# A fused attention + two-layer FFN kernel: for units 8 to 23 the output, state, carried product and the next unit's scores become one piece, and score quarters above the diagonal are left out

## Chip, cores, metric

One core of a Trainium2 chip. The metric is device time in microseconds of one execution; three runs of the kernel before and one profiled execution are known.

## The reference

Gated linear attention with a per-channel decay, over 4 batches, 8 heads, 768 tokens and head width 48, then two feed-forward layers (384 to 2048 to 384) over the 3072 rows of 384:

```
for t in range(S):
    state = alpha[:, :, t, :, None] * state + np.einsum('bhd,bhe->bhde', k[:, :, t], v[:, :, t])
    y[:, :, t] = np.einsum('bhd,bhde->bhe', q[:, :, t], state)
...
h = x @ w_in ; g = np.maximum(0.01 * h, h) ; x = g @ w_out
h = x @ w_in ; g = np.where(h > 0.0, h, alpha * (np.exp(np.minimum(h, 0.0)) - 1.0)) ; g @ w_out
```

## The kernel before

**Units.** The 3072 tokens are cut into 24 units of 128. Six units make a batch; c is a unit's place in it, and at c = 0 no state comes in. The 8 heads go as 4 pairs, on partitions 0 to 47 and 64 to 111 (112 rows). For a unit u, VectorE (DVE) makes two scans over alpha: E from the right, whose product with the keys is kS, and F from the left, whose product with the queries is q. TensorE (PE) then makes

- the scores kS' q, in two PSUM tiles `sc0` and `sc1`. A pair's 128 keys x 128 queries of one head are two matmuls of 64 keys each (`attn_scT`), so the 48-row, 64-column matmuls of two heads and two key halves stand in four quadrants of the array: 16 matmuls a unit, 4 in each quadrant. All of the square is computed; the mask (DVE, `mask_half`, two instructions with the 0/1 tile `causal`) then clears the half above the diagonal and writes A.
- the carried product q times the state that comes in (`carried`), 8 matmuls, into the output tile `po`. It stands right behind the scores.
- `pk`, four transposes of kS; ScalarE (ACT) copies it out as `kn`.
- the output, `po` += A v (8 matmuls), and the new state's part `pu` = kn v (8 matmuls).

ACT then copies `po` out as the high part xh (three instructions), and DVE subtracts it from `po` for the low part xl (three, `attn_xl`); DVE adds the state S = pu + carried and makes the next `carried` = S pe. An fp32 matmul of these runs as two passes, which the trace counts as two instructions. Feed-forward matmuls are fp32r, 128x512, in high and low parts: three terms in place of one product.

**Order.** Four units make a block of 512 tokens, and feed-forward layer 1 runs over a block in 16 steps m. A step s issues nine hp matmuls for the step s + 2, the activation of that (ACT t, DVE max, ACT gh, DVE gl), then the attention's piece for this step, and then nine y matmuls of step s. Every engine keeps the order in which the program is written. Units 0 to 11 and layer 1 of blocks 0 and 1 stand in a list written out by hand (`STARTUP`, about 0 to 200 us); from then on the loop has three pieces for each unit in one step each (about 200 to 434 us, units 12 to 23):

```
def attn_pe(u, i):   # i: piece
    0: attn_scT(u)            (scores, carried product)
    1: attn_pk(u)
    2: attn_po(u), attn_pu(u)
def attn_post(u, i):
    0: masks of u, then E, pe, kS of u + 1
    1: kn of u, then F, q of u + 1
    2: xh, S, carried for u + 1, xl; at a block's end xl and the gather come first
```

Layer 2 (434 to 906 us) follows and is not touched. In the loop a step has one bank for hp; y has 3 banks, the pool `ps_a` ("at") has 3, and a further one, h1, takes half of `po`. In the loop sc0, sc1, `pk`, the other half of `po`, and `pu` take the three "at" banks in turn. gh has two buffers: gh of step s + 2 is written when y of step s has read its own.

**Transfers.** Unit u + 3's pack (alpha, k, q) and values vt are loaded behind piece 2 of u, one DMA each, by ACT's queue (by SP's at a block's end). At a block's end ten DMAs on SP gather the fourth group of rows into the other three (`gather`). At each batch's start a GpSimd (POOL) memset pads vt (L138); POOL also clips pe (L157).

Of the kernel before, what the change touches and what calls it, by code (L numbers as in the profile page):

```python
# [19 lines left out]
def attention_two_layers_kernel(  # L20
# [12 lines left out]
    nc = tc.nc  # L33
# [29 lines left out]
    causal = const.tile([128, C], F32, name="causal")  # L63
    minus = const.tile([PR, PR], F32R, name="minus")
# [8 lines left out]
    both = [[wts.tile([128, 2 * DM], F32R, name=f"w{i}_{m}") for i in range(2)] for m in range(KF)]  # L73
    win = [[t[:, 0:DM].rearrange("p (c f) -> p c f", f=128) for t in both[m]] for m in range(KF)]
# [10 lines left out]

    def constants():
        make_identity(nc, ident)
        nc.scalar.activation(minus, ident[0:PR, 0:PR], ACTF.Copy, scale=-1.0)
        nc.gpsimd.memset(causal, 1.0)
        nc.gpsimd.affine_select(  # L90
            out=causal, in_=causal, compare_op=ALU.is_ge, fill=0.0,
            base=0, pattern=[[1, C]], channel_multiplier=-1,
        )
# [20 lines left out]
    def load_unit(u, first=False, eng=None):  # L114
        t = pack_p.tile([PR, EXT + 2 * NP * C], F32, tag="pack", name="pack")
        if first:
            m = EXT + NP * C
            nc.sync.dma_start(t[:, 0:EXT], seqs[u, :, 0:EXT])
            nc.scalar.dma_start(t[:, EXT:m], seqs[u, :, EXT:m])
# [15 lines left out]
    def load_v(u, eng=None):  # L135
# [70 lines left out]
    def mask_half(u, j):  # L206
# [3 lines left out]
        nc.vector.tensor_mul(d["A"][:, j], d["sc"][j], causal.unsqueeze(1).to_broadcast([128, NP, C]))  # L210
# [18 lines left out]

    def attn_scT(u):  # L230
        d = st[u]
        kS, qh = d["kS"], d["qh"]
# [19 lines left out]

    def attn_po(u):
        c = u % NC
        d = st[u]
        vt = vts[u]
        A, qh = d["A"], d["qh"]
        if u < EARLY:
            d["po"] = [ps_a.tile([PR, NP, C], F32, tag="at", name="po")]
        t = d["po"]  # L260
        n = len(t)
        for p in range(NP):
            for j in range(2):
                o, dst = part(t, p, j)
                c0, wide = (3 * p + 2 * j) * D, D if o or (n == 2 and c > 0) else 64
                nc.tensor.matmul(dst[0:wide], lhsT=vt[:, c0:c0 + wide], rhs=A[:, j, p],  # L266
                                 start=(p < n and (n == 1 or c == 0)), stop=(p >= NP - n and (n == 2 or c == 0)),
                                 skip_group_check=True)
        if c > 0 and n == 1:
            for p in range(NP):  # L270
                for j in range(2):
                    r = slice(64 * j, 64 * j + D)
                    nc.tensor.matmul(t[0][r, p], lhsT=d["T"][r, p], rhs=qh[r, p],
                                     start=False, stop=(p == NP - 1), skip_group_check=True)

    def attn_pu(u):
# [138 lines left out]
    def ffn1_g(j, m):  # L415
# [6 lines left out]
        more.0 E.0 pe.0 F.0 kS.0 q.0 E.1 warm.3 sc.0 mask1.0 mask0.0 pe.1 kS.1 F.1 E.2 q.1 pe.2 kS.2 F.2 pk.0 warm.3  # L422
        po.0 kn.0 xh.0 pk.1 pu.0 warm.6 sc.1 rest.0 kn.1 S.0 xl.0 T.1 warm.2 pk.2 kn.2 mask0.1 mask1.1 pu.1 E.3 po.1
        q.2 pe.3 S.1 more.1 stage.1 F.3 kS.3 sc.2 more.3 more.2 T.2 xh.1 warm.3 rest.1 mask0.2 mask1.2 pk.3 pu.2 E.4
        q.3 pe.4 S.2 po.2 sc.3 p1.0 xl.1 F.4 kS.4 kn.3 mask1.3 mask0.3 T.3 xh.2 warm.4 rest.2 pu.3 pk.4 xl.2 kn.4
        p2.0 po.3 xh.3 E.5 q.4 sc.4 rest.3 pe.5 S.3 and.0 F.5 j1.0 kn.5 warm.2 pu.4 mask0.4 mask1.4 T.4 po.4 xl.3
        gather.0 stage.2 kS.5 j2.0 q.5 S.4 E.6 and.1 sc.5 hi.0 hA.0.0.7 p1.1 p2.1 T.5 xh.4 kS.6 mask1.5 mask0.5 pe.6
        pk.6 lo.0 F.6 j1.1 hB.0.0 rest.4 po.5 and.2 q.6 t.0.0 sc.6 max.0.0 p1.2 kn.6 xl.4 more.4 stage.3 j2.1 xh.5
        j1.2 gh.0.0 p2.2 hi.1 yA.0.0 rest.5 hA.0.1 pu.6 mask1.6 mask0.6 lo.1 E.7 hB.0.1 j2.2 kS.7 po.6 gl.0.0 pe.7
        pk.7 F.7 q.7 p2.3 S.6 hi.2 hA.0.2 yB.0.0 t.0.1 xl.5 xh.6 kn.7 T.7 p1.3 lo.2 and.3 sc.7 hB.0.2 rest.6 pu.7  # L430
        mask0.7 mask1.7 max.0.1 po.7 j1.3 j2.3 more.5 stage.4 xl.6 gh.0.1 t.0.2 yA.0.1 xh.7 hi.3 rest.7 hA.0.3
        gl.0.1 max.0.2 lo.3 xl.7 gh.0.2 gather.1 yB.0.1 yA.0.2 hB.0.3 stage.5 p2.4 p1.4 t.0.3 gl.0.2 and.4 j1.4 j2.4
        max.0.3 and.5 E.8 hA.1.0 hA.1.1 hB.1.0 stage.6 hB.1.1 yB.0.2 hA.1.2 hB.1.2 hi.4 t.1.0 t.1.1 p1.5 gh.0.3 p2.5
        t.1.2 max.1.0 pe.8 j1.5 gl.0.3 j2.5 max.1.1 lo.4 max.1.2 and.6 S.7 yA.0.3 yB.0.3 hA.1.3 p2.6 yc.0.3.0 gh.1.0
        yc.0.3.1 p1.6 yc.0.3.2 hi.5 gh.1.1 gl.1.0 j1.6 j2.6 F.8 lo.5 gl.1.1 stage.7 hA.1.4 hB.1.4 hB.1.3 yA.1.0
        and.7 t.1.3 hi.6 p1.7 gh.1.2 p2.7 t.1.4 yB.1.0 j1.7 hA.1.5 yA.1.1 hB.1.5 yB.1.1 lo.6 j2.7 gl.1.2 max.1.4
# [10 lines left out]
        hB.0.13 yA.0.9 hB.0.12 max.0.11 gl.0.9 and.15 yB.0.9 pu.8 j1.14 j2.14 gl.0.10 E.10 p2.15 t.0.13 yA.0.10
        gh.0.11 p1.15 t.0.12 kn.9 hi.14 j1.15 sc.8 yB.0.10 yA.0.11 hA.0.14 S.8 q.9 kS.10 max.0.12 lo.14 hB.0.14
        pe.10 gl.0.11 mask0.8 max.0.13 j2.15 mask1.8 carry.9 pu.9 po.8 gh.0.12 t.0.14 hi.15 gh.0.13 more.8 more.9
        gl.0.12 max.0.14 lo.15 hA.0.15 yB.0.11 hB.0.15 pk.10 yA.0.12 hA.1.8 yB.0.12 S.9 gl.0.13 sc.9 hB.1.8 yA.0.13  # L450
# [641 lines left out]
```

## Time and profile before

| | |
|---|---|
| three runs | 906.21, 907.30 (median), 908.37 us |
| profiled execution | 908.03 us |
| its span, first to last instruction | 906.2 us |
| PE busy in the span | 893.1 us |
| mean granted TensorE clock | 0.998 |

The time of an execution is its span and 1.8 us around it. The profiled execution stands 0.7 us above the median.

### The profile page before, as it was taken

To read this page: it belongs to the slowest core of one execution; us is meant where nothing else is said; L and a number is where in the kernel's file an instruction comes from. 1 tells how busy PE (TensorE), PEld (TensorE's weight loads), DVE (VectorE), ACT (ScalarE), POOL (GpSimd) and SP (SyncE) were. 2 spreads that over 40 slices of the span, in tenths; PEclk is the share of its full clock that TensorE was granted. 3 is DMA by queue.
4 is the path that set the end of the run, shared out by engine and by line. 5 is a ranking of instruction groups with operands and counts; after the bars stand their busy time and mean duration, and the time that the engine had idled before them with its cause. 6 is when DMAs were issued, how large, how long until landed. Compare 5 with 4: busy or idle time off the path is not lost.

```text
span 906.2 us, 13533 instructions
## 1 busy us (share of the span) xinstructions
PE 893.1 (99%) x5302; PEld 732.9 (81%) x5302; DVE 532.3 (59%) x878; ACT 453.2 (50%) x841; POOL 10.4 (1%) x35
## 2 busy tenths in 40 slices
PE   8999999999999999999999999999999999999997
PEld 6778887788788878888888888888888888888896
DVE  8989887746664665565488887433443443443332
ACT  3567663222233223323466888656565566466442
POOL 1000000000000000000000000000000000000000
PEclk9999999999999999999999999999999999999999
DMA  9955552221113133120433331200300300300201
GB/s 241 232 147 144 162 149 75 81 56 45 45 45 79 44 88 79 42 57 17 116 111 106 86 105 52 47 20 21 57 11 21 56 22 11 56 20 1 37 1 39
DMA packets 55049, 64.00 MB, mean 71 GB/s; under 512 B 35456, under 2 KB 35968, under 8 KB 54976
## 3 DMA queue, kind: packets, MB, share of 16 engines
q1 hardware_dynamic: 52080, 54.73, 23.6%
q10 hardware_dynamic: 2896, 8.31, 3.3%
q8 instruction: 44, 0.72, 0.3%
q14 instruction: 29, 0.24, 0.1%
HBM read 54.37 MB, written 4.72 MB: 65 GB/s over the span
## 4 chain that ended last, share of the span: by engine, by line
PE 94%; DVE 2%; DMA 2%; ACT 1%; issue 1%; SPq 1%; POOL 0%; ACTq 0%; DVEq 0%; POOLq 0%
PE y L482 22%; PE hp L521 21%; PE hp L395 20%; PE o L570 11%; PE oa L570 7%; PE oa L585 3%; PE po L266 2%; PE sc L238 2%; PE pu L285 1%; PE o L585 1%; PE hw L381 1%; PE pk L196 1%; DMA x2t<-in_w_dram 1%; DMA vt<-in_vals_dram 1%; PE sc L188 1%; PE po L246 1%
## 5 line engine op out<-in xcount | busy, mean ns | idle before, releaser
L395 PE MATMUL hp<-x,w 128*128 128x512 f32 x864 | 215.6, 391 | 0.2 <-DMA x<-x 0.2
L521 PE MATMUL hp<-x,w 128*128 128x512 f32 x864 | 212.3, 390 | 0.0
L395 PEld LDWEIGHTS hp<-x,w 128*128 128x128 f32 x864 | 161.1, 188 | 35.9 <-DMA x<-x 1.1
L521 PEld LDWEIGHTS hp<-x,w 128*128 128x128 f32 x864 | 161.8, 188 | 33.3 <-DVE w L367 0.2
L482 PE MATMUL y<-gh,w 128*128 128x512 f32 x576 | 171.6, 397 | 0.0
L534 DVE SCALAR_TENSOR_TENSOR t<-t,hp 128x512 f32<-128x512 f32 x96 | 65.9, 687 | 143.5 <-ACT t L529 143.0
L409 ACT CAST gh<-t 128x512 fp32r<-128x512 f32 x96 | 59.9, 624 | 145.9 <-PE y L482 97.1
L413 DVE TENSOR_TENSOR gl<-t,gh 128x512 fp32r<-128x512 f32 x96 | 65.9, 690 | 102.6 <-ACT gh L409 98.7
L482 PEld LDWEIGHTS y<-gh,w 128*128 128x128 f32 x576 | 105.1, 188 | 23.7 <-issue 2.8
L545 DVE TENSOR_TENSOR gl<-t,gh 128x512 fp32r<-128x512 f32 x96 | 66.5, 693 | 66.2 <-ACT gh L539 66.2
L400 ACT COPY t<-hp 128x512 f32<-128x512 f32 x96 | 56.0, 585 | 95.8 <-PE hp L395 90.7
L482 PE MATMUL y<-gl,w 128*128 128x512 f32 x288 | 102.5, 392 | 0.2 <-DVE gl L413 0.2
L528 ACT ACTIVATE t<-hp 128x512 f32<-128x512 f32 x96 | 57.2, 596 | 80.5 <-PE hp L521 80.2
L539 ACT CAST gh<-t 128x512 fp32r<-128x512 f32 x96 | 59.7, 622 | 70.3 <-PE o L570 23.1
L570 PE MATMUL o<-gh,w 128*128 128x512 f32 x288 | 88.7, 389 | 0.1
L405 DVE SCALAR_TENSOR_TENSOR t<-t 128x512 f32<-128x512 f32 x96 | 65.8, 687 | 24.7 <-ACT t L400 23.1
L482 PEld LDWEIGHTS y<-gl,w 128*128 128x128 f32 x288 | 53.7, 188 | 12.4 <-DVE gl L413 0.6
L570 PEld LDWEIGHTS o<-gh,w 128*128 128x128 f32 x288 | 54.0, 188 | 11.6 <-ACT x2t L503 0.5
L529 ACT ACTIVATE t<-t 128x512 f32<-128x512 f32 x96 | 60.7, 633 | 3.1
L570 PE MATMUL oa<-gh,w 128*128 128x512 f32 x192 | 59.1, 389 | 0.0
L570 PE MATMUL o<-gl,w 128*128 128x512 f32 x144 | 56.0, 389 | 0.0
L570 PEld LDWEIGHTS oa<-gh,w 128*128 128x128 f32 x192 | 36.0, 188 | 7.5
(130 smaller groups left out, 883.1 us busy)
## 6 DMA issues: line engine op xcount, KB each, us to landing
stg<-in_w_dram SPq DMA_DIRECT2D x28, 384.0 KB, 3.1
pack<-in_seqs_dram SPq DMA_DIRECT2D x14, 674.2 KB, 6.2
x2t<-in_w_dram SPq DMA_DIRECT2D x20, 384.0 KB, 3.7
span<-in_seqs_dram SPq DMA_DIRECT2D x24, 226.2 KB, 2.6
vt<-in_vals_dram SPq DMA_DIRECT2D x17, 288.0 KB, 7.2
pack<-in_seqs_dram ACTq DMA_DIRECT2D x7, 674.2 KB, 5.0
x2t<-in_w_dram SPq DMA_DIRECT2D x32, 144.0 KB, 2.8
out_dram<-osb SPq DMA_DIRECT2D x60, 64.0 KB, 2.0
```

The lines of the kernel that those rows point to most:

```text
L395: nc.tensor.matmul(hp, lhsT=a[:, kk, :], rhs=x[:, kk, :n], start=(0 in halves and i == 0), stop=(1 in halves and i == len(terms) - 1))
L405: nc.vector.scalar_tensor_tensor(out=t, in0=t, scalar=0.01, in1=t, op0=ALU.mult, op1=ALU.max)
L409: nc.scalar.copy(gh, steps["t", j, m])
L413: nc.vector.tensor_sub(gl, steps.pop(("t", j, m)), steps["gh", j, m].bitcast(F32))
L482: nc.tensor.matmul(ytiles[j][c], lhsT=a[:, c * 128:(c + 1) * 128], rhs=x, start=(first and 0 in halves and c not in begun), stop=(last and ...
L521: nc.tensor.matmul(hp, lhsT=a[:, kk, :], rhs=x[:, kk, :], start=(i == 0), stop=(i == 3 * KD - 1))
L528: nc.scalar.activation(t, hp, ACTF.Relu, scale=-1.0)
L529: nc.scalar.activation(t, t, ACTF.Exp, scale=-1.0)
L534: nc.vector.scalar_tensor_tensor(out=t, in0=t, scalar=-1.0, in1=hp, op0=ALU.add, op1=ALU.max)
L539: nc.scalar.copy(gh, t)
L545: nc.vector.tensor_sub(gl, t, gh.bitcast(F32))
L570: nc.tensor.matmul(otiles[j][c], lhsT=a[:, c * 128:(c + 1) * 128], rhs=x, start=(m == 0 and i == 0), stop=(m == KF - 1 and i == 2),)
```

## The change

In units 8 to 23 there are still three pieces, but the PE work is in two: piece 0 is `pk`, piece 1 has none, and piece 2 is a new function, `attn_X`, that issues output, state part, carried product and the scores of the next unit, one behind the other. The two score tiles are allocated once and stay; they hold two of the three "at" banks, and the third is shared by the low half of `po` and by `pk`. `pu` lies in h1 behind po's other half. For units above 8, of each pair's two key halves one is computed for the later 64 queries only; in pairs 2 and 3 the key halves are swapped (by the loads, and by E read in reverse), so that each quadrant has two whole and two half matmuls. The mask is a bitwise and, with an int32 tile `keep`, and it is done one piece earlier, behind `attn_X` of the unit before. Loads for units from 8 on are 4 + 3 DMAs, all on SP. The POOL memset on vt is gone, `minus` lies in a weight tile, and `STARTUP` is written anew as a whole, the early units too.

```
-    causal = const.tile([128, C], F32, name="causal")
-    minus = const.tile([PR, PR], F32R, name="minus")
+    keep = const.tile([128, 2, C], I32, name="keep")
...
         else:
-            (eng or nc.sync).dma_start(t, seqs[u])
+            m, e = EXT + 2 * C, EXT + NP * C
+            nc.sync.dma_start(t[:, 0:m], seqs[u, :, 0:m])
+            dst, src = [a.rearrange("r (g h c) -> r g h c", g=2, h=2) for a in (t[:, m:e], seqs[u, :, m:e])]
+            for h in range(2):
+                nc.sync.dma_start(dst[:, :, h], src[:, :, 1 - h])
+            nc.sync.dma_start(t[:, e:], seqs[u, :, e:])
...
-        t = v_p.tile([128, NP * 3 * D + 16], F32, tag="v", name="vt")
-        if u >= EARLY and u % NC == 0:
-            nc.gpsimd.memset(t[:, NP * 3 * D:], 0.0)
-        (eng or nc.sync).dma_start(t[:, 0:NP * 3 * D], vals[u])
+        t = v_p.tile([128, NP * 3 * D], F32, tag="v", name="vt")
...
+            dst, src = [a.rearrange("k (g e) -> k g e", g=NP) for a in (t[:, 0:NP * 3 * D], vals[u])]
+            nc.sync.dma_start(dst[:, 2:4], src[:, 1::-1])
+            for h in range(2):
+                nc.sync.dma_start(dst[64 * h:64 * h + 64, 0:2], src[64 - 64 * h:128 - 64 * h, 2:4])
...
+        for i in range(2):
+            k, e = [a.rearrange("r g (h c) -> r g h c", h=2) for a in (d["kS"][:, 2 * i:2 * i + 2], e2[:, 2 * i:2 * i + 2, 1:C + 1])]
+            nc.vector.tensor_mul(k, k, e[:, :, ::-1] if i else e)
...
-        nc.vector.tensor_mul(d["A"][:, j], d["sc"][j], causal.unsqueeze(1).to_broadcast([128, NP, C]))
...
+        nc.vector.tensor_tensor(out=a, in0=s, in1=m, op=ALU.bitwise_and)
...
+    scores = []
     def attn_scT(u):
...
-        sc = [ps_a.tile([128, NP, C], F32, tag="at", name=f"sc{j}") for j in range(2)]
+        if not scores:
+            scores.extend(ps_a.tile([128, NP, C], F32, tag="at", name=f"sc{j}") for j in range(2))
         for p in range(NP):
-            for i in range(2):
+            for i in (p > 0, p == 0):
+                late = 64 if u > EARLY and i != p // 2 else 0
                 for j in range(2):
                     r, o = slice(64 * j, 64 * j + D), slice(64 * i, 64 * i + 64)
-                    nc.tensor.matmul(sc[j][o, p], lhsT=kS[r, p, o], rhs=qh[r, p, :], start=True, stop=True)
+                    nc.tensor.matmul(scores[j][o, p, late:], lhsT=d["kS"][r, p, o], rhs=d["qh"][r, p, late:],
+                                     start=True, stop=True)
...
+    def attn_X(u):
+        d = st[u]
+        c = u % NC
+        low = ps_a.tile([PR, 2, C], F32, tag="at", name="po")
+        bank = ps_h.tile([PR, 2 * C + NP * D], F32, tag="h1", name="po")
+        t = d["po"] = [low, bank[:, 0:2 * C].rearrange("k (g c) -> k g c", c=C)]
+        for p in range(NP):
+            for j in range(2):
+                o, dst = part(t, p, j)
+                c0, wide = vcol(u, p, j), D if o else 64
+                nc.tensor.matmul(dst[0:wide], lhsT=vts[u][:, c0:c0 + wide], rhs=d["A"][:, j, p],
+                                 start=(p < 2), stop=(p >= 2 and c == 0), skip_group_check=True)
+        if c < NC - 1:
+            attn_pu(u, bank[:, 2 * C:].rearrange("k (g e) -> k g e", e=D))
+        if c > 0:
...
+                    nc.tensor.matmul(dst, lhsT=carried[r, p * D:p * D + (D if o else 64)], rhs=d["qh"][r, p],
+                                     start=False, stop=(p >= 2), skip_group_check=True)
+        if u + 1 < NU:
+            attn_scT(u + 1)
...
     def attn_pe(u, i):
         if i == 0:
-            attn_scT(u)
-        elif i == 1:
             attn_pk(u)
-        else:
-            attn_po(u)
-            attn_pu(u)
+        elif i == 2:
+            attn_X(u)
     def attn_post(u, i):
         last = u + 1 == NU
         if i == 0:
-            attn_mask(u)
+            attn_kn(u)
...
         elif i == 1:
-            attn_kn(u)
...
+            attn_state(u)
             attn_xh(u, xh, off)
             ends = u == blocks[j][0] + blocks[j][1] - 1
             if ends:
                 attn_xl(u, xh, xl, off)
                 gather(t, blocks[j][1] * C, swapped=True)
-            attn_state(u)
             if not last:
+                attn_mask(u + 1)
                 attn_carry(u + 1)
             if not ends:
                 attn_xl(u, xh, xl, off)
             st.pop(u)
-            next_load(u + 3, nc.sync if ends else nc.scalar)
+            next_load(u + 3)
```

On DVE, first the step of the output of unit 12 in the kernel before: gl of the step, then the state, the carried state, and the three low parts; the masks come a step of their own later.

```order
L413 TENSOR_TENSOR gl<-t,gh 128x512
L321 TENSOR_TENSOR S<-pu,carried 112x192
L228 TENSOR_TENSOR carried<-S,pe 112x192
L306 TENSOR_TENSOR x<-po,x 112x2x128
L306 TENSOR_TENSOR x2t_141<-po,x2t_141 112x128
L306 TENSOR_TENSOR x<-po,x 112x128
L405 SCALAR_TENSOR_TENSOR t<-t 128x512
L413 TENSOR_TENSOR gl<-t,gh 128x512
L210 TENSOR_TENSOR A<-sc_2607,causal 128x512
L210 TENSOR_TENSOR A<-sc_2608,causal 128x512
```

The same step in the changed kernel, still on DVE:

```order
L464 TENSOR_TENSOR gl<-t,gh 128x512
L372 TENSOR_TENSOR S<-po,carried 112x192
L239 TENSOR_TENSOR A<-sc_1301,keep 128x512
L239 TENSOR_TENSOR A<-sc_1302,keep 128x512
L257 TENSOR_TENSOR carried<-S,pe 112x192
L357 TENSOR_TENSOR x<-po,x 112x2x128
L357 TENSOR_TENSOR x2t_140<-po,x2t_140 112x128
L357 TENSOR_TENSOR x<-po,x 112x128
L456 SCALAR_TENSOR_TENSOR t<-t 128x512
```

The two masks (now of the next unit) have moved in between the state and the low parts. The first low part, `x<-po,x 112x2x128`, is the one that reads the half of `po` in the "at" bank.

On PE, the end of that same piece of unit 12 in the changed kernel, the y matmuls between left out, and then the next step:

```order
L301 MATMUL po<-pack,carried 64x128
L274 MATMUL sc_1301<-pack 64x128
L274 MATMUL sc_1302<-pack 64x128
L274 MATMUL sc_1301<-pack 64x64
L274 MATMUL sc_1302<-pack 64x64
...
L446 MATMUL hp<-x,w_11_126 128x512
L446 MATMUL hp<-x,w_11_125 128x512
L219 MATMUL pk<-ident,pack 128x112 x4
L532 MATMUL y_2215<-gh,w_9_121 128x512
```

In the kernel before, `pk` of a unit came a step behind its scores, on PE too:

```order
L246 MATMUL po<-pack,carried 48x128 x2
L246 MATMUL po<-pack,carried 64x128
L482 MATMUL y_2175<-gh,w_9_122 128x512
...
L395 MATMUL hp<-x,w_12_129 128x512
L395 MATMUL hp<-x,w_12_128 128x512
L196 MATMUL pk<-ident,pack 128x112 x4
L482 MATMUL y_2175<-gh,w_10_124 128x512
```

The transposes of unit 13 now stand one step behind the outputs of unit 12, and they write the "at" bank in which the low half of unit 12's `po` lay; what has to be read out of it before is in the DVE rows above.

On POOL, the kernel before; the two memsets of vt stand between the clips of pe, and in the changed kernel the 24 clips are one run:

```order
L157 TENSOR_SCALAR pe<-E 112x4 x11
L138 MEMSET vt 128x16
L157 TENSOR_SCALAR pe<-E 112x4 x6
L138 MEMSET vt 128x16
L157 TENSOR_SCALAR pe<-E 112x4 x7
```

## Rows read from the trace of the kernel before

**Rows 1.** The page, part 1: busy us of each engine.

```profile
PE 893.1 (99%) x5302; PEld 732.9 (81%) x5302; DVE 532.3 (59%) x878; ACT 453.2 (50%) x841; POOL 10.4 (1%) x35
```

**Rows 2.** Windows of 25 us: busy by engine, granted clock, DMA share.

```profile
25.00:50.00 25.00, 23.98 (x266) 18.99 (x265) 24.76 (x38) 14.27 (x30) 1.66 (x3) 1.00 0.93 239
...
150.00:175.00 25.00, 23.22 (x220) 18.34 (x219) 17.63 (x34) 6.23 (x16) 0.85 (x3) 1.00 0.24 68
```

**Rows 3.** Timeline of PE, 280 to 316 us: four steps of the loop.

```profile
281.05 2.20 PE L395 MATMUL hp<-x,w 128*128 128x512 f32 x9
...
285.13 2.20 PE L395 MATMUL hp<-x,w 128*128 128x512 f32 x9
287.26 1.11 PE L238 MATMUL sc<-pack 48*64 48x128 f32 x32
288.19 0.61 PE L246 MATMUL po<-pack,carried 48*64 48x128 f32 x16
...
290.91 2.20 PE L395 MATMUL hp<-x,w 128*128 128x512 f32 x9
292.98 0.57 PE L196 MATMUL pk<-ident,pack 112*128 112x112 f32 x4
...
295.49 2.21 PE L395 MATMUL hp<-x,w 128*128 128x512 f32 x9
297.62 1.08 PE L266 MATMUL po<-A,vt 128*48 128x128 f32 x16
298.54 0.61 PE L285 MATMUL pu<-vt,kn 128*64 128x48 f32 x16
...
301.25 2.20 PE L395 MATMUL hp<-x,w 128*128 128x512 f32 x9
```

**Rows 4.** Timeline of PE, 23.5 to 45 us: outputs, then the early carried product T.

```profile
29.50 1.09 PE L266 MATMUL po<-A,vt 128*64 128x128 f32 x16
30.52 1.08 PE L273 MATMUL po<-x2t,T 48*48 48x128 f32 x16
```

**Rows 5.** Timeline of PE, 160.5 to 162 us: pu and po side by side.

```profile
161.25 0.30 PE L266 MATMUL po<-A,vt 128*48 128x128 f32 x1
161.29 0.22 PE L285 MATMUL pu<-vt,kn 128*64 128x48 f32 x1
```

**Rows 6.** Timeline of DVE, 301 to 312 us: behind the output of a unit; idle before in brackets.

```profile
301.88 0.69 DVE L413 TENSOR_TENSOR gl<-t,gh 128x512 fp32r<-128x512 f32 x1 [1.67 <-ACT gh L409]
302.49 0.35 DVE L321 TENSOR_TENSOR S<-pu,carried 112x192 f32<-112x192 f32 x1
302.88 0.36 DVE L228 TENSOR_TENSOR carried<-S,pe 112x192 f32<-112x192 f32 x1
303.15 0.42 DVE L306 TENSOR_TENSOR x<-po,x 112x256 fp32r<-112x256 f32 x1
...
308.28 1.28 DVE L210 TENSOR_TENSOR A<-sc,causal 128x512 f32<-128x512 f32 x2
309.48 1.23 DVE L151 TENSOR_TENSOR_SCAN E<-pack,d 112x517 f32<-112x517 f32 x1
```

**Rows 7.** Timelines of POOL, DVE and PE, 160 to 175 us: a chain of waits.

```profile
162.46 0.11 POOL L138 MEMSET vt<- 128x16 f32 x1 [25.18 <-PE po L266]
...
162.79 1.23 DVE L151 TENSOR_TENSOR_SCAN E<-pack,d 112x517 f32<-112x517 f32 x1 [2.52 <-POOL pe L157]
...
173.58 1.08 PE L266 MATMUL po<-A,vt 128*48 128x128 f32 x16 [1.78 <-DVE A L210]
```

**Rows 8.** Timelines of SP and PE, 269 to 279 us, and the page's DMA issues.

```profile
273.56 2.71 SPq L334 DMA_DIRECT2D x<-x  x4
...
276.97 2.20 PE L395 MATMUL hp<-x,w 128*128 128x512 f32 x9
...
pack<-in_seqs_dram ACTq DMA_DIRECT2D x7, 674.2 KB, 5.0
...
x<-x SPq DMA_DIRECT2D x30, 64.0 KB, 2.3
```

More of the change, by code (lines that the diff above doesn't have):

```diff
@@ L83, in split, with causal @@
         (lo_engine or nc.vector).tensor_sub(lo, src, dst.bitcast(F32))
+    def causal(odd):
+        bits = keep[:, odd]
+        nc.gpsimd.memset(bits, -1)
+        for i in range(1 + odd):
+            part = bits[64 * i:64 * i + 64] if odd else bits
+            nc.gpsimd.affine_select(
+                out=part, in_=part, compare_op=ALU.is_ge, fill=0,
+                base=-64 * (odd - i), pattern=[[1, C]], channel_multiplier=-1,
+            )
     def constants():
@@ L88, in constants @@
         nc.scalar.activation(minus, ident[0:PR, 0:PR], ACTF.Copy, scale=-1.0)
[L89 to L93, printed above, removed]
+        causal(0)
+        causal(1)
         nc.vector.memset(d0, 0.0)
@@ L112, in attention_two_layers_kernel, with load_unit @@
     st = {}
-    def load_unit(u, first=False, eng=None):
+    def load_unit(u, first=False):
         t = pack_p.tile([PR, EXT + 2 * NP * C], F32, tag="pack", name="pack")
@@ L209, in mask_half @@
             d["A"] = at_p.tile([128, 2, NP, C], F32, tag="A", name="A")
-        nc.vector.tensor_mul(d["A"][:, j], d["sc"][j], causal.unsqueeze(1).to_broadcast([128, NP, C]))
+        a, s, m = d["A"][:, j].bitcast(I32), d["sc"][j].bitcast(I32), keep
+        if u < EARLY:
+            m = m[:, 0].unsqueeze(1).to_broadcast([128, NP, C])
+        else:
+            a, s = [z.rearrange("k (i g) c -> k i g c", i=2) for z in (a, s)]
+            m = m.unsqueeze(2).to_broadcast([128, 2, NP // 2, C])
+        nc.vector.tensor_tensor(out=a, in0=s, in1=m, op=ALU.bitwise_and)
     def attn_mask(u):
@@ L245, in attn_scT @@
                     r = slice(64 * j, 64 * j + D)
-                    nc.tensor.matmul(dst, lhsT=carried[r, p * D:p * D + (D if o else 64)], rhs=qh[r, p],
-                                     start=(p < 2), stop=False, skip_group_check=True)
-    def part(t, p, j):
-        o = j ^ (p % len(t))
-        return o, t[p % len(t)][64 * o:64 * o + (D if o else 64), p // len(t)]
+                    nc.tensor.matmul(dst, lhsT=carried[r, p * D:p * D + (D if o else 64)], rhs=d["qh"][r, p],
+                                     start=False, stop=(p >= 2), skip_group_check=True)
+        if u + 1 < NU:
+            attn_scT(u + 1)
     def attn_po(u):
@@ L255, in attn_po @@
         d = st[u]
[L256 to L261, printed above, removed]
+        t = ps_a.tile([PR, NP, C], F32, tag="at", name="po")
+        d["po"] = [t]
         for p in range(NP):
             for j in range(2):
[L264 to L269, printed above, removed]
+                o, dst = part(d["po"], p, j)
+                c0, wide = vcol(u, p, j), D if o else 64
+                nc.tensor.matmul(dst, lhsT=vts[u][:, c0:c0 + wide], rhs=d["A"][:, j, p],
+                                 start=(p == 0), stop=(p == NP - 1 and c == 0), skip_group_check=True)
+        if c > 0:
             for p in range(NP):
@@ L280, in attn_pu @@
         if c < NC - 1:
-            pu = ps_a.tile([PR, NP, D], F32, tag="at", name="pu")
+            whole = pu is None
+            if whole:
+                pu = ps_a.tile([PR, NP, D], F32, tag="at", name="pu")
             for p in range(NP):
@@ L285, in attn_pu @@
                     nc.tensor.matmul(pu[r, p], lhsT=d["kn"][:, p, r],
-                                     rhs=vt[:, (3 * p + 2 * j) * D:(3 * p + 2 * j + 1) * D], start=(p == 0), stop=(p == NP - 1),
+                                     rhs=vt[:, vcol(u, p, j):vcol(u, p, j) + D],
+                                     start=(whole and p == 0), stop=(p == NP - 1),
                                      skip_group_check=True)
@@ L421, in attention_two_layers_kernel @@
     STARTUP = """
[L422 to L436, printed above, removed]
@@ L447, in attention_two_layers_kernel @@
[L447 to L450, printed above, removed]
-        t.0.15 kn.10 xh.8 t.1.8 gh.0.14 hA.1.9 yB.0.13 yA.0.14 E.11 xl.8 carry.10 gl.0.14 mask1.9 max.0.15 mask0.9
@@ L457, in attention_two_layers_kernel @@
-        hA.1.15 t.1.14 hB.1.15 yB.1.11 gh.1.12 t.1.15 more.10 more.11 gh.1.13 gl.1.12 max.1.14 gl.1.13 F.12 q.12
-        max.1.15 gather.2 yA.1.12 hA.2.0 yB.1.12 hB.2.0 yA.1.13 t.2.0 gh.1.14 gh.1.15 yB.1.13 hA.2.1 hB.2.1 gl.1.15
-        yA.1.14 gl.1.14 yB.1.14 max.2.0 yA.1.15 yB.1.15 gh.2.0 t.2.1 gl.2.0 max.2.1 yc.1.15.0 gh.2.1 gl.2.1
-        yc.1.15.1 yc.1.15.2
+        more.0 E.0 pe.0 F.0 kS.0 q.0 warm.4 sc.0 E.1 mask0.0 pe.1 mask1.0 kS.1 F.1 E.2 q.1 pe.2 kS.2 F.2 pk.0 kn.0
+        warm.2 pu.0 po.0 pk.1 kn.1 S.0 xh.0 warm.6 sc.1 rest.0 warm.3 pu.1 pk.2 T.1 xl.0 mask0.1 mask1.1 po.1 E.3
@@ new lines, in attention_two_layers_kernel @@
+        q.2 S.1 pe.3 kS.3 F.3 sc.2 kn.2 xh.1 T.2 rest.1 warm.3 pu.2 pk.3 mask0.2 mask1.2 q.3 S.2 E.4 and.0 sc.3 po.2
+        more.1 xl.1 p1.0 p2.0 kn.3 kS.4 mask1.3 mask0.3 pe.4 T.3 xh.2 po.3 pu.3 stage.1 more.2 E.5 F.4 xh.3 kS.5 S.3
+        q.4 pe.5 j1.0 F.5 rest.2 rest.3 pk.4 warm.1 sc.4 mask1.4 q.5 mask0.4 xl.2 xl.3 gather.0 kn.4 p2.1 T.4 p1.1
+        warm.8 sc.5 po.4 pu.4 stage.2 more.4 more.3 stage.3 E.6 j2.0 pe.6 mask1.5 mask0.5 and.1 S.4 kS.6 hi.0 xh.4
+        T.5 hA.0.0.7 lo.0 rest.4 pk.6 hB.0.0 po.5 xl.4 t.0.0 kn.6 F.6 j1.1 and.2 q.6 max.0.0 j2.1 sc.6 E.7 gh.0.0
@@ new lines, in attention_two_layers_kernel @@
+        mask0.6 mask1.6 xh.5 p1.2 p2.2 hi.1 pe.7 j1.2 kS.7 j2.2 F.7 lo.1 q.7 yA.0.0 pu.6 po.6 rest.5 hA.0.1 xh.6 S.6
+        hi.2 rest.6 pk.7 hA.0.2 sc.7 xl.6 kn.7 xl.5 p1.3 and.3 lo.2 hB.0.1 hB.0.2 mask0.7 mask1.7 j1.3 pu.7 T.7 p2.3
+        t.0.2 t.0.1 j2.3 gl.0.0 po.7 yB.0.0 hi.3 xh.7 hA.0.3 stage.4 more.5 stage.5 rest.7 and.4 max.0.1 lo.3
+        max.0.2 p1.4 gh.0.1 xl.7 gh.0.2 E.8 gl.0.1 gl.0.2 kS.8 j1.4 yA.0.1 hB.0.3 yB.0.1 yA.0.2 p2.4 gather.1 p1.5
+        t.0.3 pk.8 yB.0.2 hA.1.0 j2.4 max.0.3 pe.8 and.5 j1.5 stage.6 hB.1.0 gh.0.3 hi.4 t.1.0 p2.5 hA.1.1 hB.1.1
```

78 lines of the change are left out of this document (50 added, 28 removed).

## The prediction

> **What bounds the kernel now.** I read the busy times first: PE is busy for 893.1 us, and the profiled execution's span is 906.2 us [rows 1]; DVE and ACT have about half of that. So in most of the program time is what PE issues, and an engine beside it counts only where PE waits for it. Two windows show where that is otherwise [rows 2]: in 25 to 50 us DVE is busy for 24.76 of 25 us and PE for less, so in the start of the hand-written list DVE sets the pace; in 150 to 175 us PE lacks 1.78 us, and that is one wait, for a mask A on DVE, ahead of the outputs at 173.58 [rows 7]. The granted clock stays at 1.00 in that window, so a wait of this size costs its own length and nothing behind it.
>
> The loop's steps give the prices [rows 3]. A plain step lasts from the first hp at 281.05 to that at 285.13: 4.08 us. The step with scores and carried product lasts 5.78 (285.13 to 290.91), so 1.70 more; that with pk 4.58, so 0.50 more; that with outputs and pu 5.76 (295.49 to 301.25), so 1.68 more. Nothing in these four steps waits: an attention piece costs just what stands in PE's stream.
>
> **The change part by part.**
>
> *One stint for two.* The scores are 32 instructions in 0.93 us until the carried product starts (287.26 to 288.19), four abreast: 8 rounds of 0.116 [rows 3]. The 16 carried ones make 4 rounds more. Twelve rounds by 0.116 are 1.39 of the 1.70 us; by 0.11, if the first round has a start of its own, 1.32. So going from the wide matmuls into the narrow ones and back costs 0.31 to 0.38; I take 0.35. Each stint that goes saves that. By the program there are 34 stints with scores, outputs or pu in units 8 to 23 before (10 in the list, 24 in the loop) and 17 after (16 pieces X and the first scores): 17 x 0.35 = 5.95 saved. In X the matmuls go once from 128 rows to 64 rows inside the stint. The nearest row: 16 outputs followed by T, with such a change, take 1.02 us (29.50 to 30.52) [rows 4], and 16 outputs followed by pu, without one, 0.92 (297.62 to 298.54) [rows 3]; that is 0.10 each time, 16 x 0.10 = 1.6 lost. Net -4.35.
>
> *Half quarters.* For units 9 to 23, each quadrant has two whole and two half matmuls in place of four whole ones, in two passes: of 8 rounds, four shrink to half. If the quadrants run on their own, that is 2 x 0.11 = 0.22 a unit, 15 x 0.22 = 3.3 saved. If the four abreast had to stay in step, nothing is saved, since in every round one of them is whole. What speaks for their own pace: at 161.25 an output matmul (48 columns wide) starts ahead of the last pu (161.29, 64 wide), though all pu stand ahead of po in the program [rows 5]. Column groups thus run ahead of each other. I take -3.3, bounds 0 and -3.3.
>
> The Trainium skill, "PSUM — Partial Sum Buffer", section "Engine vs sequencer instructions", says that TensorE's matmuls start and complete in program order. By that, four neighbours could not drift apart, the saving would be near 0 and the sum 3.3 us higher; the two rows just named show starts out of that order, so I go with the rows and keep the rule as a rival.
>
> *The POOL memset.* It waited 25.18 us for a PE output and stood ahead of a clip of pe; E on DVE waited 2.52 us for that clip, and at the end of this line PE waited the 1.78 us [rows 7]. The memset is gone: -1.8, bounds 0 (DVE late for another reason) and -1.8.
>
> *What DVE does behind X.* This is the new cost. pk is a step behind X, in the "at" bank that the low half of po had, so PE must wait there until DVE has read it with the first low part (and ACT with xh, which that needs). Before, behind the output step: the next hp starts at 301.25, gl at 301.88, S at 302.49, carried at 302.88, the first low part at 303.15 for 0.42 [rows 6]. Now two masks come in between, which take 1.20 from 308.28 to 309.48 [rows 6] (a bitwise and in place of a product, same tile and same source; I take the same time). So, from the hp on: gl 0.63, S 1.24, masks 1.63 to 2.83, carried to 3.10, low part to 3.52. pk would stand 2.07 behind the hp (290.91 to 292.98) [rows 3]. The wait is 1.45. It holds for the units whose pk comes right behind an X inside a block: 13, 14, 15, 18, 19, 21 and 22. For 12, 16 and 20 the low parts of the block's last unit come first. Unit 18 starts a batch: no S and no carried, 0.39 and 0.27 less, so 0.8. Sum 6 x 1.45 + 0.8 = 9.5. Behind pk, the y matmuls and all later steps are late by the same; nothing gives it back, since PE has no other idle time in the loop. It would be 0 if pk got a bank that is free, and 10.2 at most, if unit 18 cost the full 1.45.
>
> *pk, masks, E in the loop.* pk itself is as long as before, and piece 1 now has no PE work; the number of pk stays. The masks leave their old place, so E, kS and the rest come earlier there. kS is two instructions of half size. DVE is busy for only 17.63 of 25 us in the window of 150 to 175, which still has the list's work in it [rows 2], so idle time of DVE hides them: 0. Were that cover gone, the further instruction might cost what carried takes, the shortest pitch in [rows 6], 0.27, in 12 units 3 us. Scores for u + 1 need q of u + 1, which is made in the step ahead: gl comes 0.63 behind the hp and takes 0.61, F (a scan as E is) 1.2 and q (a product of the same width as gl) 0.6 [rows 6]: ready 3.1 us behind that hp, while X's scores come a whole step later: 0.
>
> *Loads.* In place of 1 + 1 DMAs there are 4 + 3, all on SP, whose queue in the loop has only these and the gathers. A pack took 5.0 us from issue to landing [rows 8]. Seven issues of some 0.6 us (two in 1.22, four in 2.71 us on SP are the nearest) [rows 8] make 4 us of issuing more. The unit's E comes more than three steps (over 12 us) later: 0. At a block's end they stand behind the gather, as before.
>
> *Gather.* S is now ahead of the low parts at a block's end, so the gather starts 0.39 later [rows 6]. Its last four issues run from 273.56 to 276.27 and a landing takes 2.3 [rows 8], so the last is there about 277.9; the next block's hp start at 276.97, and need the last group in the seventh matmul, 1.4 us later, at 278.3. The slack is 0.4: 0 to 0.1, three times, +0.2.
>
> *The list.* It is written anew, and what it gives can't be read from rows. Its first 45 us are bound by DVE [rows 2], and DVE's instructions ahead of the first converted weight are the same set in another order. From there PE is full. By the order, the pk of units 9 and 10 wait for low parts too, with other matmuls ahead of them. I take +0.5, bounds -3 (as much PE idle as 25 to 50 and 150 to 175 us have between them, 1.02 + 1.78) and +3 (two waits of 1.45).
>
> **Sum.** -4.35 - 3.3 - 1.8 + 9.5 + 0.2 + 0.5 = +0.75. The profiled execution has 908.03 us (its span 906.2 and 1.8 around it); so has it 908.8 after. It stood 0.7 above the median of the three runs, so the median should go from 907.3 to 908.1.
>
> **Rivals.**
> - *The wait at pk is hidden or absent* (the low part comes earlier than my chain says, or pk has another bank). For: DVE has much idle time in the loop. Against: all of the chain ahead of the low part hangs on gl, which waits for ACT, which waits for PE's y [rows 6], so it can't start earlier. 908.1 - 9.5 = 898.6, faster. At a wait of under 0.9 a unit in place of 1.45 the change is measurably faster.
> - *Quarters don't shorten* (the quadrants stay in step): 908.1 + 3.3 = 911.4, slower. The row of pu and po speaks against it, but it shows two column groups, not four quadrants.
> - *The list brings new waits:* in X of units 8 to 11 everything hangs on masks, state and kn in one place; two such waits, and 911.1, slower.
> - *The list is better by 3 us:* 905.1, faster.
>
> **Chances.** My forecast, with its own range of 905 to 911, has 0.60; hidden wait 0.13; quarters in step 0.10; a worse list 0.10; a better list 0.07. About 0.2% (1.8 us) is what can be told from no change: 905.5 to 909.1. Faster: 0.13 + 0.07 and 0.04 of the forecast's lower end, 0.24. Slower: 0.10 + 0.10 and 0.20 of its upper end (the list is uncertain to 3 us), 0.40. Same: 0.36. The range, 901.5 to 912.5, leaves out the fully hidden wait (0.13) and a few in the hundred where two losses meet; a half-hidden wait (903.4) is in it.
>
> **What would show it.** In the loop of the changed kernel: steps with X of about 4.08 + 2.9 (1.70 + 1.68 - 0.35 + 0.10 - 0.22) = 7.0 us; steps with pk of 4.6 + 1.45 = 6.0, with PE idle ahead of pk for the DVE's low part, in seven units; no such wait at 12, 16 and 20; no wait of PE near 173 us; in X the scores taking about 0.7 us in place of 0.93. I am wrong if PE doesn't wait at pk, if X's scores last as long as before, or if units 0 to 11 end more than 3 us from where they did.

## The result

The changed kernel takes 919.4 us (median of 6 runs, 916.1 to 922.2) against 907.3 before (906.2 to 908.8): ratio 1.013 (95% interval 1.0102 to 1.0157), 12 us slower. The profiled execution has 920.86 us, its span 919.1. The forecast was 908.1, with 912.5 as its upper end.

The page, part 1, of the changed kernel, and its longest waits of PE:

```profile
PE 892.4 (97%) x5306; PEld 735.0 (80%) x5306; DVE 531.4 (58%) x894; ACT 455.6 (50%) x841; POOL 11.8 (1%) x36
```

```profile
PE pk L219 <- DVE x L357: 8.7, 7, 1.3
PE hp L446 <- DMA x<-x: 2.6, 1, 2.6
PE hw L432 <- ACT w L98: 2.5, 1, 2.5
PE pk L219 <- DVE S L372: 1.7, 1, 1.7
```

PE is busy for 0.7 us less than before [rows 1], in a span that is 12.9 longer. The first wait is the forecast one, in seven units. The second was not forecast.

Where the time went is read from the starts of hp matmuls at the same place of both kernels (us from the span's start):

| | before | changed | later by |
|---|---|---|---|
| first hp of layer 1 | 39.74 | 44.93 | 5.2 |
| first hp of block 1 | 65.48 | 73.32 | 7.8 |
| first hp of block 2 | 193.99 | 201.67 | 7.7 |
| first hp of layer 2 | 501.52 | 514.28 | 12.8 |

The loop loses 5.1 us, all that lies ahead of block 2 loses 7.7. Of the 5.2 us that are lost ahead of the first hp, PE's idle time has 2.8 (7.1 against 4.3 us) and a lower granted clock 1.7 (the last section has the row); this stretch also differs from run to run, as shown below. In the loop the steps look like this (timeline of PE, 237 to 250 us, X of a unit and the step behind it):

```profile
237.88 2.20 PE L446 MATMUL hp<-x,w 128*128 128x512 f32 x9
240.01 1.09 PE L292 MATMUL po<-A,vt 128*64 128x128 f32 x16
240.93 0.62 PE L335 MATMUL po<-vt,kn 128*48 128x48 f32 x16
241.48 0.67 PE L301 MATMUL po<-pack,carried 48*64 48x128 f32 x16
241.96 0.86 PE L274 MATMUL sc<-pack 48*64 48x64 f32 x32
...
244.92 2.20 PE L446 MATMUL hp<-x,w 128*128 128x512 f32 x9
248.45 0.57 PE L219 MATMUL pk<-ident,pack 112*128 112x112 f32 x4 [1.33 <-DVE x L357]
```

X's step lasts 7.04 us (237.88 to 244.92; 7.0 forecast), and pk starts 3.53 us behind the hp of its step (244.92 to 248.45) in place of 2.07 [rows 3]: 1.46 lost (1.45 forecast). The DVE rows for the same place, against [rows 6]:

```profile
245.55 0.69 DVE L464 TENSOR_TENSOR gl<-t,gh 128x512 fp32r<-128x512 f32 x1 [3.57 <-ACT gh L460]
246.16 0.35 DVE L372 TENSOR_TENSOR S<-po,carried 112x192 f32<-112x192 f32 x1
246.43 1.28 DVE L239 TENSOR_TENSOR A<-sc,keep 128x512 int32<-128x512 int32 x2
247.62 0.34 DVE L257 TENSOR_TENSOR carried<-S,pe 112x192 f32<-112x192 f32 x1
247.89 0.41 DVE L357 TENSOR_TENSOR x<-po,x 112x256 fp32r<-112x256 f32 x1
```

The two masks stand between the state and the low part, whose end at 248.30 lets pk go at 248.45.

In the list, SP and PE of the changed kernel, 56 to 74 us (the second number of an SP row is the time in issuing):

```profile
57.12 0.37 SPq L135 DMA_DIRECT2D pack<-in_seqs_dram  x1
57.54 4.92 SPq L138 DMA_DIRECT2D pack<-in_seqs_dram  x2
62.50 0.46 SPq L139 DMA_DIRECT2D pack<-in_seqs_dram  x1
...
64.78 0.52 SPq L720 DMA_DIRECT2D x2t<-in_w_dram  x1
...
67.69 0.42 SPq L722 DMA_DIRECT2D x2t<-in_w_dram  x1
68.83 1.97 SPq L385 DMA_DIRECT2D x<-x  x3
```

```profile
73.32 2.15 PE L446 MATMUL hp<-x,w 128*128 128x512 f32 x4 [2.55 <-DMA x<-x]
```

The two key transfers of unit 8 (L138) write strips of the tile that lie between each other; they are called interleaved below. They keep SP for 4.92 us. The transfers of the next group of layer-1 weights (stage 5, L720 to L722) are then issued only at 64.78 to 67.69, right ahead of the gather of block 1, whose six transfers take 4.3 to 5.0 us to land, and PE waits for them. That the one leads to the other is tested in runs 4 to 9.

### The profile page after: what moved, and what is told of

It reads as the page before. It is cut to its first block, busy times and chain, and to the rows that moved or that the text cites. A ratio compares the mean times of both kernels' runs of the same rounds, so it can differ in the third digit from the quotient of the medians.

```text
span 919.1 us, 13668 instructions
## 1 busy us (share of the span) xinstructions
PE 892.4 (97%) x5306; PEld 735.0 (80%) x5306; DVE 531.4 (58%) x894; ACT 455.6 (50%) x841; POOL 11.8 (1%) x36
## 4 chain that ended last, share of the span: by engine, by line
PE 82%; DVE 7%; DMA 6%; ACT 2%; SPq 1%; issue 1%; POOL 0%; DVEq 0%; ACTq 0%; POOLq 0%
PE hp L571 21%; PE y L532 17%; PE hp L446 16%; PE o L620 11%; PE oa L620 7%; PE oa L635 3%; DMA x2t<-in_w_dram 2%; PE po L292 2%; DMA vt<-in_vals_dram 2%; DMA pack<-in_seqs_dram 2%; PE sc L274 1%; DVE A L239 1%; DVE gl L464 1%; PE o L635 1%; ACT gh L460 1%
```

## The experiments

Each run is named in brackets as the expectations name it. Ratios are to the kernel before on the same chip, with 95% intervals, and us over or under the kernel before are that ratio on 907.3. From here on "list" is the time from the first hp of layer 1 to the first of block 2, without the stretch ahead of it, and "loop" that from there to the first of block 5 (by then all attention is done), in the profiled executions. Before: list 154.3, loop 242.2. Changed: list 156.7, loop 247.3.

**1. The loop alone (loop_alone).** The list of before (units 0 to 11, with its pieces and loads), `XU = 12` in place of `EARLY` in the new conditions, the scores of unit 12 put into the list:

```
-        elif u < EARLY:
+        elif u < XU:
...
-    hB.2.0 yA.1.13
+    hB.2.0 sc.12 yA.1.13
```

> Units 0 to 11 go by the list of before, with its pieces and loads; from unit 12 on the loop is that of the changed kernel (X, half quarters, masks ahead of the low parts). The scores of unit 12 are a stint of their own in the list, and the POOL memset is gone. Theory: the changed loop alone costs what its steps showed, 5.1 us from the first to the last loop step, the score stint of unit 12 moves into the list (1.3), and the wait at 173 us goes (-1.8): 907.3 + 4.6 = 911.9, and the list ends where it did before. Rival: the loss lies in the loop's loads or in a state that the loop brings about (clock, transfers), and then this is near 919.

913.0 us, ratio 1.0051 (1.0025 to 1.0078), 4.6 us over: as expected. Loop 248.6. PE no longer waits between 110 and 200 us, where it had the 1.78 [rows 7].

**2. The same, low parts ahead of the masks (loop_alone_xl).**

```
-            if not last:
-                attn_mask(u + 1)
-                attn_carry(u + 1)
             if not ends:
                 attn_xl(u, xh, xl, off)
+            if not last:
+                attn_mask(u + 1)
+                attn_carry(u + 1)
```

> As the one above, with the low parts ahead of the masks on VectorE. Theory (pk waits for the first low part because the masks stand ahead of it): the seven waits of 1.45 and 0.8 go, 911.9 - 9.5 = 902.4, and pk's steps last 4.58 again. Rival (pk waits for something else of X, such as gl or the copy xh, and the low part is only last): the waits shrink by less than half, 907 or more.

904.1 us, ratio 0.9949 (0.9930 to 0.9968). The loop takes 239.05 in place of 248.59: 9.5 back, the forecast sum. In its timeline of PE, pk stands 2.07 behind the hp, with nothing waited for, and its step lasts 4.56:

```profile
240.78 2.20 PE L489 MATMUL hp<-x,w 128*128 128x512 f32 x9
242.85 0.57 PE L220 MATMUL pk<-ident,pack 112*128 112x112 f32 x4
245.34 2.20 PE L489 MATMUL hp<-x,w 128*128 128x512 f32 x9
```

**3. The changed kernel with that one edit (xl_first).**

> The changed kernel with the low parts ahead of the masks, its list as it is. Theory: 919.4 - 9.5 = 909.9, and the list still ends some 8 us later than before. Rival: the waits at pk cover others, and at most half comes back: 914 or more.

908.3 us, ratio 0.9988 (0.9970 to 1.0006). Loop 237.8 in place of 247.3, again 9.5; list 157.2, still late. The wait of 2.5 for the gathered rows is still there.

**4. Plain loads (plain_loads).** One pack transfer and two for the values, no swap, so whole quarters:

```
-            for h in range(2):
-                nc.sync.dma_start(dst[:, :, h], src[:, :, 1 - h])
-            nc.sync.dma_start(t[:, e:], seqs[u, :, e:])
+            nc.sync.dma_start(t, seqs[u])
...
-                late = 64 if u > EARLY and i != p // 2 else 0
+                late = 0
```

> The changed kernel with the pack of a unit loaded by one transfer and the values by two, no swapped key halves, so all score quarters whole and kS in one instruction. Leaves out nothing of the computation. Theory A (the many small transfers on the sync queue make the list late): 3.3 more for the quarters, and most of the 8 us of the list back: 914 to 917. Theory B (the order of the new list makes it late whatever the loads): 919.4 + 3.3 = 922.7, with the gather of block 1 as late as in the changed kernel.

913.8 us, ratio 1.0059 (1.0038 to 1.0081): 5.4 over: theory A, a little under its 6.7 to 9.7. The list takes 150.8 in place of 156.7, and no hp waits for the gather.

**5. The swap done in the layout of the inputs (host_swap).** Half quarters stay; a unit's pack and values are one transfer each.

```
-            dst, src = [a.rearrange("r (g h c) -> r g h c", g=2, h=2) for a in (t[:, m:e], seqs[u, :, m:e])]
-            for h in range(2):
-                nc.sync.dma_start(dst[:, :, h], src[:, :, 1 - h])
+            nc.sync.dma_start(t, seqs[u])
...
+    late = kq[8:, :, 0, 2:].copy()
+    kq[8:, :, 0, 2:, 0:64], kq[8:, :, 0, 2:, 64:] = late[..., 64:], late[..., 0:64]
...
+    vals[8:, :, 2], vals[8:, :, 3] = late[:, :, 1], late[:, :, 0]
+    vals[8:, 0:64, 0:2], vals[8:, 64:, 0:2] = late[:, 64:, 2:4], late[:, 0:64, 2:4]
```

> The changed kernel with everything as it is (list, X, half quarters, masks ahead of the low parts), but the key halves and the value pairs are swapped in the layout of the inputs, so that each unit's pack and values are one whole transfer each on the sync queue. Theory (the small transfers hold up the sync queue, the fifth stage of weights then collides with the gather of block 1, and PE waits there): the first hp of block 1 waits no more, the list gets some 6 us back: 12 over the kernel before becomes about 6. Rival (the new list is late by its order, and whole quarters had moved the work in plain_loads): 11 to 12 over, as the changed kernel.

912.7 us, ratio 1.0059 (1.0042 to 1.0076); list 151.4. So the swap itself costs nothing here, its transfers do; 5.4 over in place of 11.8.

**6. The same, low parts first (host_swap_xl)**, by the edit of run 2.

> host_swap with the low parts ahead of the masks. Theory: both losses gone, what is left is the gain of the stints, the quarters and the POOL wait: 6 over less 9.5, 3 to 6 us under the kernel before. Rival: a loss of the list's order that the runs so far can't tell from the transfers' spread stays: same as before or slower.

901.5 us, ratio 0.9938 (0.9916 to 0.9960), 5.6 under.

**7. Small transfers in the kernel before (before_small)**, cut into the four of the changed kernel:

```
-            (eng or nc.sync).dma_start(t, seqs[u])
+                e_.dma_start(t[:, 0:m], seqs[u, :, 0:m])
...
+                for h in range(2):
+                    e_.dma_start(dst[:, :, h], src[:, :, h])
+                e_.dma_start(t[:, e:], seqs[u, :, e:])
```

> The kernel before, with the pack of each unit from 8 on cut into the four transfers of the changed kernel (same pieces, nothing swapped), on the queues of before. Theory (it is the collision with the gather that costs, not small transfers as such): in the list of before they are issued some 17 us ahead of the gather of block 1, so 0 to 2 us. Rival (small transfers cost time wherever they stand, on the 16 DMA engines or at the queue): 4 us or more.

915.4 us, ratio 1.0101 (1.0063 to 1.0140): both expectations missed the place. The list is as before (154.3), so the small pieces cost nothing there. The loop takes 248.0, 5.8 more. The loads of the loop are on ACT's queue in that kernel; ACT rows around one of them:

```profile
305.73 0.44 ACTq L133 DMA_DIRECT2D pack<-in_seqs_dram  x1
...
308.82 0.33 ACTq L133 DMA_DIRECT2D pack<-in_seqs_dram  x1
309.19 0.47 ACTq L134 DMA_DIRECT2D pack<-in_seqs_dram  x1
309.70 0.44 ACTq L148 DMA_DIRECT2D vt<-in_vals_dram  x1
310.18 0.59 ACT L409 COPY t<-hp 128x512 f32<-128x512 f32 x1 [3.78 <-issue]
```

Between the two key transfers (L133) the queue stands still for 2.65 us (306.17 to 308.82), and ACT, which also computes, is idle for 3.78 us before its next copy. PE's waits in this run have six of some 0.5 us ahead of pk, for a mask on DVE, 2.9 in all; the kernel before has one, of 0.4, in its list.

**8. The two key transfers of unit 8 on ACT's queue (keys8_on_act).**

```
-                nc.sync.dma_start(dst[:, :, h], src[:, :, 1 - h])
+                (nc.scalar if u == 8 else nc.sync).dma_start(dst[:, :, h], src[:, :, 1 - h])
```

> The changed kernel with the two small key transfers of unit 8 alone on ScalarE's queue. Theory (the sync queue stands still behind them): the sync queue doesn't stop behind the pack of unit 8, stage 5 is issued some 4 us earlier, the gather lands in about 3 us in place of 4.4 to 5 and the wait ahead of block 1's first hp falls below 1 us: 3 to 5 us less than the changed kernel, so 7 to 9 over the kernel before. Rival (the transfers themselves take the DMA engines' time): the wait stays at 2 us or more, 11 to 12 over.

919.7 us, ratio 1.0140 (1.0123 to 1.0157), by the number the rival. The trace says otherwise: stage 5 goes out at 60.17 to 61.96 and the gather lands in 2.4 to 2.9 us (4.3 to 5.0 in the changed kernel), as the theory has it. But ACT stands still instead, and PE's y waits 4.0 us for its gh:

```profile
60.99 4.85 ACTq L138 DMA_DIRECT2D pack<-in_seqs_dram  x2
66.02 0.89 ACT L392 ACTIVATE x2t<-x2t 128x768 f32<-128x768 f32 x1 [4.45 <-DMA pack<-in_seqs_dram]
```

The first of the two landed at 65.50, and the second was issued at 65.52. The stop travels with the pair of transfers. The waits in the built program of the changed kernel say why (SP, unit 8; DMAHW0 to 7 count landings, and each transfer counts on one of them in turn and waits for its own from the time before):

```
50 L138 DMA pack<-in_seqs_dram 112x2x64 [waits DMAHW4_49]
51 L138 DMA pack<-in_seqs_dram 112x2x64 [waits DMAHW5_49,DMAHW4_49]
```

The second has one wait more, on the count of the first. Their targets lie between each other in the tile (halves h = 0 and h = 1 of two pairs), and the program orders them. In the program of run 9 below no key transfer waits for another's landing.

**9. The same small pieces, not interleaved (keys_by_pair).**

```
-            for h in range(2):
-                nc.sync.dma_start(dst[:, :, h], src[:, :, 1 - h])
+            for g in range(2):
+                for h in range(2):
+                    nc.sync.dma_start(dst[:, g, h], src[:, g, 1 - h])
```

> The changed kernel, with the two interleaved key transfers (each half of both pairs) replaced by four, one for each pair and half: the same small pieces, but none lies between the pieces of another, so the program puts no wait of one upon another's landing. Theory (it is this wait, for which the issuing queue stands still some 4.5 us, that makes the fifth weight stage meet the gather): the sync queue issues without the stop, the list is 4 to 6 us shorter than the changed kernel's, 6 to 8 over the kernel before in all. Rival (the small pieces take the time as such): 11 to 13 over, as the changed kernel.

910.9 us, ratio 1.0041 (1.0024 to 1.0059), 3.7 over in place of 11.8: 8 us less, more than the theory's 4 to 6. The list takes 148.9 in place of 156.7. SP issues four pieces in 1.83 us, the gather goes out at 63.38 and no hp waits for it:

```profile
54.15 0.37 SPq L135 DMA_DIRECT2D pack<-in_seqs_dram  x1
54.57 1.83 SPq L139 DMA_DIRECT2D pack<-in_seqs_dram  x4
56.45 0.42 SPq L140 DMA_DIRECT2D pack<-in_seqs_dram  x1
...
63.38 2.07 SPq L386 DMA_DIRECT2D x<-x  x3
```

```profile
67.71 5.64 PE L447 MATMUL hp<-x,w 128*128 128x512 f32 x24
```

**10. Whole quarters (whole_quarters).**

```
-                late = 64 if u > EARLY and i != p // 2 else 0
+                late = 0
```

> xl_first with all score quarters whole (the swaps stay as they are). Theory (quadrants run on their own): 0.19 to 0.22 more in each X with scores, 15 units, 3 us over xl_first, 2 to 3 over the kernel before, and X's step goes from 7.04 to about 7.25. Rival (the four stay in step): as xl_first, same as the kernel before.

The kernel that ran was that of run 6 with `late = 0`, not xl_first as the expectation names it, so it is compared with run 6: 906.6 us, ratio 0.9978 (0.9962 to 0.9993) against 0.9938 (0.9916 to 0.9960), 3.6 us more. X's step is 7.28 (292.27 to 299.55; 7.25 at most other places) in place of 7.04, and the scores take 1.07 in place of 0.85 to 0.86:

```profile
292.27 2.20 PE L438 MATMUL hp<-x,w 128*128 128x512 f32 x9
...
296.35 1.07 PE L266 MATMUL sc<-pack 48*64 48x128 f32 x32
299.55 2.21 PE L438 MATMUL hp<-x,w 128*128 128x512 f32 x9
```

**11. The gather as early as before (host_swap_xl_gather).** The kernel of run 6, and:

```
-            attn_state(u)
             attn_xh(u, xh, off)
...
                 gather(t, blocks[j][1] * C, swapped=True)
+            attn_state(u)
```

> host_swap_xl with the state behind the low parts at a block's end too, so that the gather goes out as early as in the kernel before. Theory: the three steps that wait 0.4 for the gathered rows last 4.08 again, 1.2 us less than host_swap_xl, 6.5 to 7 under the kernel before. Rival (the 0.4 comes from the transfers themselves): no change against host_swap_xl, 5.5 under.

902.2 us, ratio 0.9931 (0.9914 to 0.9947). The loop takes 236.7 in place of 237.7, and the step at the first hp of block 3 lasts 4.08 (275.67 to 279.75) in place of 4.43 (275.27 to 279.70). So the 0.4 was the state ahead of the gather; in the ratio it can't be told.

**12. Both waits undone in the changed kernel itself (both_waits_gone)**, by the edits of runs 9, 2 and 11:

> The changed kernel with its two waits undone and all else kept: four key transfers that don't lie between each other (as keys_by_pair), the low parts ahead of the masks, and at a block's end ahead of the state too. Theory (the two waits are all that made the change slower): keys_by_pair, 3.7 over the kernel before, less 9.5 for pk and less 1.2 for the gather, 7 under it. Rival (a third loss in the list's order shows once the two are gone): 0 to 4 under.

899.7 us, ratio 0.9899 (0.9877 to 0.9921): 9 us under the kernel before (7 were expected), and the lowest ratio of all, though its interval overlaps that of run 11. The list takes 150.3, the loop 236.8.

## Why the prediction was wrong, by its steps

*The step that failed is "Loads": "0".* I costed seven issues of some 0.6 us, and asked only whether the data come in time for the unit that uses them. I did not ask what the second interleaved key transfer waits for, nor what stands behind it on SP. It waits for the first one's landing, and SP stands still for up to 4.9 us. My sentence that SP has only loads and gathers spoke of the loop; in the list, weight stages and half of the gather go by the same queue. Undone alone (run 9), 8 of the 12 us go (1.3% less 0.41%); by the profiled executions the list gets 7.9 shorter. Of these, 2.55 are the wait for the gather; 1.7 are other waits of PE in the list, for conversions and activations (4.2 idle in all, none in run 9); 1.7 are a lower granted clock (below); and some 2 are matmuls that lasted longer, which no run takes apart. Other pairs of kernels put the price lower: 6.4 (the changed kernel and run 5), 4.5 (runs 3 and 6), about 7 (runs 3 and 12, less the gather). That small pieces as such, or the number of packets, cost the time is excluded: run 9 has more of both, and run 7's list has the pieces for nothing. Without this loss the range would have held: run 9 is 3.7 over, and the upper end was 5.2 over.

*What DVE does behind X: 9.5.* Right in mechanism, place, size and count: seven waits (six of 1.31 to 1.33 idle us, one of 0.80), and undoing them gives back 9.5 us of the loop in two pairs of kernels (runs 1 and 2; the changed kernel and run 3).

*One stint for two and half quarters.* X's step came out at 7.04 (7.0 forecast). Undoing the half quarters costs 0.21 to 0.24 an X, 0.22 forecast, so the quadrants do not stay in step. The starts in the changed kernel's trace show it too: in one X a quadrant with halves starts four passes at 241.96 to 242.13, while its neighbour with whole ones starts two, at 241.97 and 242.08. The prediction's rival stood beside the Trainium skill's "PSUM — Partial Sum Buffer", section "Engine vs sequencer instructions"; the rival's outcome, no saving, did not come, and no run here bears the rule out, that matmuls start and complete in program order, for matmuls in different quadrants. The Trainium skill's "TensorEngine Tiling (Array Packing)", section "Key Properties", says that different tiles can execute in parallel and independently; run 10 agrees, with its 0.21 to 0.24 us.

*The POOL memset: -1.8.* PE has no such wait near 173 us, and none between 110 and 200 us in run 1, with the list of before; no run takes out the memset alone.

*Gather: +0.2.* Mis-sized: 0.4 at two block starts (steps of 4.49 and 4.50 us in place of 4.08), 0.8.

*Scores need q: 0.* One X at a batch's end has no pu ahead of its carried product, and its scores waited 0.14 us; its step was 6.97 where X less pu would be 6.6 (7.04 less 0.55, and 0.10 for the change of rows). Some 0.4 lost.

*The list: +0.5, from -3 to +3.* Without the interleaved waits the new list takes 148.9 to 151.4 us from the first hp to the loop, in seven kernels, where that of before takes 151.99 to 154.31 in four: 150.5 against 153.7 in the mean, so it keeps most of what stints, quarters and the POOL wait were to give. The stretch up to the first hp lasts 42.0 to 44.9 us with the new list (ten profiled executions) and 39.7 to 43.7 with the old (four, runs 1, 2 and 7 among them). The means, 43.1 and 41.2, are 2 us apart, but the ranges overlap: the stretch changes from execution to execution, and falls of the granted clock alone take 0, 1.7 or 3.4 us of it, with either list. Whether the order there costs 2 us stays open.

Summed anew: the forecast +0.75, 8 for SP's wait, 0.6 more for the gather and 0.4 for q give 9.8; measured are 11.8 (1.3% of 907.3, 9.3 to 14.2). The 2 that lack are as much as the open first stretch; by the lower prices for SP's wait, 2 to 5 lack. The same sum without SP's wait gives 1.75 over for run 9 and 7.75 under for run 6, where 3.7 over (2.2 to 5.4) and 5.6 under (3.6 to 7.6) were measured, so 2 lack there too. In run 12 the sum is 8.55 under and the measurement 9.2 (7.2 to 11.2): there nothing lacks. So the two waits carry most of the loss, and a third one of about 2 us is neither shown nor excluded.

## What to carry to other kernels

A transfer cut into strided pieces that lie between each other in one tile can be ordered by the program, one behind the other's landing (4.9 us on SP here, against 1.83 for the same pieces as four transfers). Look at the waits of the issuing queue, and cut so that each piece's range is its own. Whatever stands behind such a transfer on its queue is part of its price, other units' transfers and, on a computing engine's queue, that engine's work. A work item that is done earlier (the masks) displaces what stood there; what frees a buffer goes first.

## What the runs showed that was not expected

Windows of the changed kernel, the first ahead of the first hp, the other two behind the wait for the gather (the number before the last two is the granted clock):

```profile
35.00:40.00 5.00, 5.00 (x38) 3.88 (x38) 3.56 (x6) 2.40 (x7) 0.00 (x0) 0.66 0.84 166
70.00:75.00 5.00, 2.45 (x8) 1.24 (x7) 1.25 (x4) 1.57 (x3) 0.00 (x0) 0.86 0.78 195
75.00:80.00 5.00, 5.00 (x20) 3.96 (x19) 2.43 (x4) 2.70 (x5) 0.00 (x0) 0.80 0.29 79
```

Behind the idle time of PE at 70 to 73 us the granted clock falls to a mean of 0.86 and 0.80 of the full 2.4 GHz, so part of these stretches ran at 1.2 GHz; missing clock of 0.14 and 0.20 in 5 us each is some 1.7 us more than the wait itself. The same 1.7 is missing in the lists of runs 3 and 8, whose waits there were 2.5 and 4.0 us, and in no list of the new order without interleaved transfers. The 0.66 of 35 to 40 us is 1.7 us as well; PE was busy there, and idle for part of the 5 us before. In the kernel before a wait of 1.78 left it at 1.00 [rows 2, 7], and so did the six of 1.33 in the loop here. The prediction's "costs its own length and nothing behind it" holds for those, not for a wait of 2.55. Nor does the length of a wait decide it alone: in run 2 one of 1.25 us (48.61 to 49.86), with matmuls of the attention on both sides, was followed by a granted clock of 0.55 at 52 to 53 us and 0.50 at 53 to 55, again 1.7 us in all.
